# A fused RWKV and mixture-of-experts kernel: three weight splits and the sort move ahead of the second expand group

## The chip, the core and the metric

The kernel runs on one core of one Trainium2 chip. A core has five engines that each work through a queue of their own in order: TensorE (PE in the profile, with its weight loads as PEld), VectorE (DVE), ScalarE (ACT), GpSimd (POOL) and SyncE (SP), which here only starts transfers. Engines wait for each other by semaphores. The metric is device time in microseconds, the median of several runs.

## The reference

```python
def _attn_ref(r, k, v, w, u):            # batch 4, heads 8, seq 768, head_dim 48
    for t in range(S):
        cur = np.einsum('bhd,bhe->bhde', u[None] * kt, vt)
        y[:, :, t] = np.einsum('bhd,bhde->bhe', rt, state + cur)
        state = wt[:, :, :, None] * state + np.einsum('bhd,bhe->bhde', kt, vt)

def _moe_ref(x, w_gate, w1, w2):         # 3072 tokens of 384, 8 experts, hidden 1024
    logits = x @ w_gate
    expert_idx = np.argmax(logits, axis=1)
    ...
    for e in range(E):
        xe = x[expert_idx == e]
        out[expert_idx == e] = gate_w * (np.maximum(xe @ w1[e], 0.0) @ w2[e])
```

A recurrence over 768 steps gives 3072 token rows of 384. Each row goes to the one expert with its largest logit, and the result is scaled by that expert's probability.

## The kernel before

**Two stages.** The first stage works through 24 blocks of the recurrence (`iteration`), turns their outputs into token rows, computes the logits of finished groups (`logit_mm`, `gate`), numbers the rows within their expert (`rank` on TensorE, `place` on VectorE) and writes each block's 128 rows with an indirect transfer from GpSimd into a table `xs`, one region per expert (`scatter`, L603). The second stage goes through the experts one after the other. The busiest expert so far is chosen early (`choose`) and taken first; the order of the other seven is found by `sort_experts` (L632 to L637) after the last block has been ranked, for it needs the final counts (`base`, L580).

**One expert.** Its rows come back from `xs` (`rows_of`, `load_rows`, L260) and are transposed (L300). `expand` (L311) makes one of eight hidden slices of 128: nine TensorE products (three depth slices j, each as high x high, high x low and low x high parts) into one PSUM bank. ScalarE then writes the rectified high part (`hh`, L313), VectorE the rest (`hl`, L314). `contract` (L325) multiplies the eight slices by w2. The first expert's rows are taken in two parts: `ua`, the first 256 rows, known early, and `ub_`, the next 208, which can only be loaded when all blocks have been scattered.

**Splits.** A weight piece arrives by SyncE as 128 x 1536 numbers. `split_part` cuts 512 columns of it into two parts: ScalarE copies the high part (L237), VectorE subtracts to get the low part (L239). `side()` takes the next split from a list; when a piece is done, `feed()` lets SyncE load the next one. The six w1 splits of an expert come in the order set in `feed`:

```python
for k, p in ((0, 0), (0, 2), (1, 1), (0, 1), (1, 0), (1, 2)):
    sides.append(("split", e, k, (halfway["st"], st)[k], p, p == (1, 2)[k]))
```

They are called splits 1 to 6 here. Splits 1 to 3 hold the columns of hidden slices f = 0 to 3 (one split for each j), splits 4 to 6 those of f = 4 to 7. Splits 1 to 3 are done before `mm1(ua, 0)`. Splits 7 to 12 are those of w2; the w2 piece of splits 10 to 12 is the one that `feed` starts to load when split 4 is done.

**Order.** The block is inside `tc.manual_schedule` for TensorE, VectorE, ScalarE and GpSimd, and SyncE is ordered by hand as well: each engine does its instructions in the order in which the program names them. So what `side(0)` adds stands in ScalarE's and VectorE's queues just where the call is, between the `hh` and `hl` of the `mm1` calls around it. TensorE has nothing of a split in its queue. The PSUM banks of `expand` go round a list of five (`bk["b"]`): `mm1(ua, 5)` takes the bank of f = 0 again, f = 6 that of f = 1, f = 7 that of f = 2, and TensorE waits there until `hh` and `hl` of the older slice have been read out. `expert_of(order[...])` lets SyncE read the second expert's number; behind it in SyncE's queue stand the loads of `ub_` (which wait for every scatter) and of the second expert's w1 (L224).

**The first part of the first expert.** `mm1(ua, f)` is `expand` for slice f of `ua`. Between the eight of them and `contract` of `ua` there is no other TensorE work; the transpositions of `ub_` stand behind the first of the two contractions (`tick`).

Of the kernel before, what the change touches and what calls it, by code (L numbers as in the profile page):

```python
# [55 lines left out]
def rwkv_moe_kernel(ctx, tc, rkw, vv, ub, wg, wr, w1, w2, out):  # L56
# [34 lines left out]
    def misc(name):  # L91
        return psM.tile([P, BANK], F32, name=name, tag="m")
# [137 lines left out]
    def split_part(t, st, i, p, half="hl", n=3):  # L230
        nm = "w1" if i < 2 else "w2"
        k = 1536 // n
        cs = slice(p * k, (p + 1) * k)
        hi = t[nm, "h"][:, i % 2, cs]
        lo = t[nm, "l"][:, i % 2, cs]
        if "h" in half:
            nc.scalar.activation(hi, st[:, cs], AF.Copy)  # L237
        if "l" in half:
            nc.vector.tensor_tensor(out=lo, in0=st[:, cs], in1=hi.bitcast(F32), op=ALU.subtract)  # L239
# [64 lines left out]
    def expand(wt, f, x, n, hs):  # L304
        hh, hl = h_tiles(n)
        hp = turn("b", n)
        i = 0
        for j in range(3):
            wh, wl = w1v(wt, "h", j, f), w1v(wt, "l", j, f)
            for a, p in ((wh, 0), (wh, 1), (wl, 0)):  # L310
                nc.tensor.matmul(hp, a, x[p][:, j, :], start=(i == 0), stop=(i == 8))  # L311
                i += 1
        nc.scalar.activation(hh, hp, AF.Relu)  # L313
        nc.vector.scalar_tensor_tensor(out=hl, in0=hp, scalar=0.0, in1=hh.bitcast(F32), op0=ALU.max, op1=ALU.subtract)  # L314
        hs.append((hh, hl))
# [252 lines left out]
    def rank(k):  # L568
        G, i, m = k
        oh = ch["r", k][0]  # L570
        t = misc("rank")
        rk = t[:, 0:(m + 1) * E].rearrange("p (b e) -> p b e", e=E)
        ch["rank", k] = rk
        nc.tensor.matmul(rk, one32, ch["base"].unsqueeze(1).broadcast_to([1, m + 1, E]), start=True, stop=False, skip_group_check=True)
        nc.tensor.matmul(rk[:, 0:m], tri, oh, start=False, stop=False, skip_group_check=True)
        for b in range(m):
            nc.tensor.matmul(rk[:, b + 1:], ones, oh[:, b:b + 1, :].broadcast_to([P, m - b, E]),
                             start=False, stop=(b == m - 1), skip_group_check=True)
        ch["base"] = nb = sm.tile([1, E], F32, name="base", tag="base", bufs=3)
        nc.scalar.activation(nb, rk[0:1, m, :], AF.Copy)  # L580
# [12 lines left out]
    def weigh(k):  # L593
        G, i, m = k
        nc.vector.tensor_reduce(out=ch["xr", G][:, i:i + m, DM], in_=ch["r", k][1], axis=AX.X, op=ALU.add)
# [4 lines left out]
    def scatter(G, bs, behind=None):  # L600
        xr = ch["xr", G]
        for b in bs:
            i = nc.gpsimd.indirect_dma_start(out=xsf, out_offset=bass.IndirectOffsetOnAxis(ap=ch["pi", G, b], axis=0),  # L603
                                             in_=xr[:, b, :], in_offset=None, bounds_check=E * NTOK - 1, oob_is_err=False)
            if behind is not None:
                after(i, behind, "TensorE's dense products")
            for k in scat:
                tc.declare_no_dep(i.ins, k, reason="rows of different tokens")
            scat.append(i.ins)
            nc.gpsimd.memset(none, 0.0)  # L610
# [19 lines left out]
    def sort_experts():  # L630
        key = keys()
        nc.vector.tensor_tensor(out=key, in0=key, in1=pen, op=ALU.add)  # L632
        ch["ks"] = ks = sm.tile([1, E], F32, name="ks", tag="ks")
        nc.vector.max(out=ks, in_=key)
        ki = sm.tile([1, E], I32, name="ki", tag="ki")
        nc.vector.tensor_copy(ki, ks)
        nc.vector.tensor_single_scalar(out=order, in_=ki, scalar=E - 1, op=ALU.bitwise_and)  # L637
# [3 lines left out]
    def check_counts():  # L641
        ks = ch["ks"]
        nc.vector.tensor_tensor(out=bad[:, 0:E], in0=ks, in1=capk, op=ALU.is_ge)
        nc.vector.tensor_tensor(out=bad[:, E:2 * E], in0=ks, in1=leastk, op=ALU.is_lt)
        tot = sm.tile([1, 1], F32, name="tot", tag="tot")
        nc.vector.tensor_reduce(out=tot, in_=ch["base"], axis=AX.X, op=ALU.add)
        nc.vector.tensor_single_scalar(out=bad[:, 2 * E:2 * E + 1], in_=tot, scalar=float(NTOK + NTOK * E * (E - 1) // 2),
                                       op=ALU.not_equal)
# [8 lines left out]
    def check_w(i, t, h):  # L657
        th = t[:, h * 768:(h + 1) * 768]
        nc.vector.tensor_reduce(out=wck[:, 2 * i + h, 0:1], in_=th, axis=AX.X, op=ALU.min)
        nc.scalar.activation(th, th, AF.Relu, bias=mone, scale=1.0, accum_out=wck[:, 2 * i + h, 1:2])  # L660
# [129 lines left out]
    def feed():  # L790
        while len(out_) < 3:
            if not todo or todo[0][0] not in eid:
                return
            e, i = todo.pop(0)
            st = load_piece(eid[e], i) if i < 4 else load_w(e - 1)
            out_.append((e, i))
            if i == 0:
                halfway["st"] = st
            elif i == 1:
                for k, p in ((0, 0), (0, 2), (1, 1), (0, 1), (1, 0), (1, 2)):  # L800
                    sides.append(("split", e, k, (halfway["st"], st)[k], p, p == (1, 2)[k]))
            else:
                for p in range(3 if i < 4 else 2):
                    sides.append(("split" if i < 4 else "check", e, i, st, p, p == (2 if i < 4 else 1)))

    def side(limit=E):
        if sides and sides[0][1] <= limit:
            kind, e, i, t, p, done = sides.pop(0)
            if kind == "split":
                split_part(wts[e % 2], t, i, p)  # L810
            else:
                check_w(e - 1, t, p)
            if done:
                out_.remove((e, i))
                feed()
# [33 lines left out]
    with tc.manual_schedule(engines={ET.PE, ET.DVE, ET.Activation, ET.Pool}):  # L849
# [6 lines left out]
        ua, z = ch["ua"], NB - 1  # L856
# [27 lines left out]
        def mm1(u, f):  # L884
            expand(wts[u["e"] % 2], f, u["x"], u["n"], u["hs"])
# [7 lines left out]
        penalty()  # L893
        scatter(last, (0, 1, 2))
        mm1(ua, 0)
        rank(kb)
        weigh(kb)
        place(kb)
        scatter(last, (3,))
        side(0)  # L900
        mm1(ua, 1)
        side(0)
        mm1(ua, 2)
        side(0)
        sort_experts()
        eid[1] = expert_of(order[0:1, 0:1])
        ub_ = rows_of(HB, HA, 0)
        feed()
        for f in range(3, 8):
            mm1(ua, f)  # L910
            side(0)
            if f == 5:
                check_counts()
        actx.close()
# [299 lines left out]
```

## Time and profile before

| what | us |
|---|---|
| median of 3 runs | 391.16 (390.44 to 392.19) |
| the profiled execution | 389.0 |
| its span, first to last instruction | 387.3 |

Times of rows count from the start of the span. A row of the timeline gives the start, the duration (of all of them, where several are merged), engine, line, operation, tiles and count, and in brackets the idle time of the engine before it with what ended it. Ends of TensorE's products are modelled in the profile, the ends of the other engines are recorded.

### The profile page before, as it was taken

What the parts mean: (1) busy time and instruction counts of PE and PEld (TensorE: products, weight loads), DVE (VectorE), ACT (ScalarE), POOL (GpSimd) and SP (SyncE); (2) the same over time, 40 slices, a digit from 0 to 9 for tenths busy, and PEclk for the clock granted to TensorE, in tenths of its full rate; (3) what the DMA queues carried; (4) which work ended last, traced back from release to release, by engine and by line L of the source; (5) the groups of instructions that cost most, each with busy time, mean ns of one, the idle gap of its engine ahead of it and who ended that gap; (6) DMA issues with size and microseconds to landing.
All of it is one profiled execution on the core that took longest, in us unless ns stands there. A gap on an engine that the chain in (4) does not pass through costs nothing.

```text
span 387.3 us, 11609 instructions
## 1 busy us (share of the span) xinstructions
PE 360.6 (93%) x4644; PEld 326.1 (84%) x4645; DVE 261.6 (68%) x451; ACT 196.0 (51%) x516; POOL 143.8 (37%) x195
## 2 busy tenths in 40 slices
PE   7988999999998896999999999999999999999991
PEld 5666777777776675998998999999999999999990
DVE  8789999989998436595665376476476585782410
ACT  3665666566666234374454355465565563751200
POOL 5577688788887171111000130130130262124021
PEclk9999999999999696999999999999999999999996
DMA  7997777677768125977444554754764665811001
GB/s 205 261 276 215 225 209 225 202 218 220 221 179 278 50 111 146 284 244 239 117 164 162 151 155 149 224 161 154 226 172 146 208 164 187 248 70 40 20 19 41
DMA packets 38021, 67.63 MB, mean 175 GB/s; under 512 B 8141, under 2 KB 19714, under 8 KB 37962
## 3 DMA queue, kind: packets, MB, share of 16 engines
q1 hardware_dynamic: 31658, 57.33, 50.2%
q0 software_dynamic: 6304, 9.50, 7.7%
q8 instruction: 38, 0.62, 0.7%
q14 instruction: 21, 0.17, 0.1%
HBM read 55.34 MB, written 11.64 MB: 173 GB/s over the span
## 4 chain that ended last, share of the span: by engine, by line
PE 80%; DVE 7%; ACT 4%; issue 3%; POOL 2%; another core or an unknown queue 1%; DMA 1%; POOLq 0%; DVEq 0%; ACTq 0%
PE N L311 15%; PE N L325 14%; PE cell L311 7%; PE mM L311 6%; PE N L994 6%; PE cell L994 4%; PE mM L994 3%; PE yp L489 3%; PE yp L479 3%; PE ap L464 2%; DVE kh L368 2%; PE U L499 2%; PE N L300 2%; PE ap L527 2%; PE wrm L142 2%
## 5 line engine op out<-in xcount | busy, mean ns | idle before, releaser
L275 POOL DMA_INDIRECT out_dram<-ot,gi x16 | 22.2, 1391 | 104.0 <-issue 71.7
L275 POOL DMA_INDIRECT out_dram<-ort,gi x13 | 15.5, 1195 | 76.9 <-issue 19.3
L325 PE MATMUL N<-w2h,hh 128*128 128x384 f32 (+4 forms) x104 | 35.9, 345 | 0.0
L314 DVE SCALAR_TENSOR_TENSOR hl<-N,hh 128x256 fp32r<-128x256 f32 (+8 forms) x38 | 19.8, 522 | 23.7 <-ACT hh L313 21.9
L325 PE MATMUL N<-w2l,hh 128*128 128x384 f32 (+4 forms) x104 | 35.0, 337 | 0.0
L325 PE MATMUL N<-w2h,hl 128*128 128x384 f32 (+4 forms) x104 | 35.0, 337 | 0.0
L239 DVE TENSOR_TENSOR w2l<-wst,w2h 128x512 fp32r<-128x512 f32 x48 | 32.1, 687 | 4.1 <-ACT w2h L237 3.6
L239 DVE TENSOR_TENSOR w1l<-wst,w1h 128x512 fp32r<-128x512 f32 x48 | 33.1, 690 | 1.4 <-ACT w1h L237 1.0
L387 POOL TENSOR_TENSOR rk<-rkwt 112x512 f32<-112x512 f32 x24 | 30.6, 1275 | 7.8 <-DMA rkwt<-in_rkw_dram 7.8
L603 POOL DMA_INDIRECT xs<-xr,pi x24 | 24.7, 1028 | 23.8 <-issue 7.3
L313 ACT ACTIVATE hh<-N 128x256 fp32r<-128x256 f32 (+8 forms) x38 | 17.6, 464 | 27.0 <-PE N L311 22.4
L360 DVE TENSOR_TENSOR_SCAN suf<-rkwt,cell 112x536 f32<-112x536 f32 x24 | 30.4, 1267 | 0.5
L237 ACT ACTIVATE w2h<-wst 128x512 fp32r<-128x512 f32 x48 | 28.5, 625 | 3.5 <-DMA wst<-in_w_dram 3.5
L351 DVE TENSOR_TENSOR_SCAN pre<-rkwt,cell 112x536 f32<-112x536 f32 x24 | 30.2, 1259 | 0.2 <-DMA rkwt<-in_rkw_dram 0.2
L237 ACT ACTIVATE w1h<-wst 128x512 fp32r<-128x512 f32 x48 | 29.8, 623 | 0.2 <-ACT x L301 0.2
L393 POOL TENSOR_TENSOR rh<-rkwt,pre 112x512 f32<-112x512 f32 x24 | 28.9, 1203 | 2.3 <-DVE pre L351 2.0
L311 PE MATMUL N<-xh,w1h 128*128 128x440 f32 (+6 forms) x84 | 28.8, 343 | 0.0
L311 PE MATMUL N<-xh,w1l 128*128 128x440 f32 (+6 forms) x84 | 28.6, 341 | 0.0
L311 PE MATMUL N<-xl,w1h 128*128 128x440 f32 (+6 forms) x84 | 28.6, 340 | 0.0
L368 DVE TENSOR_TENSOR kh<-rkwt,suf 112x512 f32<-112x512 f32 x24 | 28.4, 1181 | 0.0
L430 ACT ACTIVATE at<-id,ct 128x64 f32<-128x64 f32 x96 | 25.3, 343 | 0.1
L373 DVE COPY_PREDICATED at<-cmask,ap 128x512 f32<-128x512 int32 x24 | 17.6, 735 | 10.2 <-PE ap L464 7.6
(200 smaller groups left out, 967.5 us busy)
## 6 DMA issues: line engine op xcount, KB each, us to landing
wst<-in_w_dram SPq DMA_DIRECT2D x48, 256.0 KB
wst<-in_w_dram SPq DMA_DIRECT2D x16, 768.0 KB
rkwt<-in_rkw_dram SPq DMA_DIRECT2D x72, 96.0 KB
rkwt<-in_rkw_dram SPq DMA_DIRECT2D x24, 238.0 KB
vt<-in_vv_dram SPq DMA_DIRECT2D x48, 96.0 KB
wck_t<-in_wr_dram SPq DMA_DIRECT2D x6, 768.0 KB
rkwt<-in_rkw_dram SPq DMA_DIRECT2D x12, 224.0 KB
xg<-xs SPq DMA_DIRECT2D x4, 579.0 KB
```

The source lines that it names most:

```text
L237: nc.scalar.activation(hi, st[:, cs], AF.Copy)
L239: nc.vector.tensor_tensor(out=lo, in0=st[:, cs], in1=hi.bitcast(F32), op=ALU.subtract)
L275: i = nc.gpsimd.indirect_dma_start(out=out[:, :], out_offset=bass.IndirectOffsetOnAxis(ap=t.bitcast(I32)[0:rows.shape[0], q, 1:2], axis=0) ...
L311: nc.tensor.matmul(hp, a, x[p][:, j, :], start=(i == 0), stop=(i == 8))
L325: nc.tensor.matmul(op, a[:, cs], w2v(wt, w, f), start=(i == 0), stop=(i == 23))
L351: nc.vector.tensor_tensor_scan(out=d["pt"][:, 0, 0:NW], data0=d["w"], data1=cell[:RP, 0:1].broadcast_to([RP, NW]), initial=1.0, op0=ALU.mu ...
L360: nc.vector.tensor_tensor_scan(out=suf[:, ::-1], data0=d["w"][:, ::-1], data1=cell[:RP, 0:1].broadcast_to([RP, NW]), initial=1.0, op0=ALU. ...
L368: nc.vector.tensor_tensor(out=d["kh"], in0=d["k"], in1=d["suf"][:, :, 3:SEG], op=ALU.mult)
L387: nc.gpsimd.tensor_tensor(out=d["rk"], in0=d["r"], in1=d["k"], op=ALU.mult)
L393: nc.gpsimd.tensor_tensor(out=d["rh"], in0=d["r"], in1=d["pre"][:, :, 1:C + 1], op=ALU.mult)
L430: nc.scalar.activation(d["at"][:, h // NQ, h % NQ, :], id2, AF.Copy, scale=d["ct"][:, h:h + 1])
L994: nc.tensor.matmul(pp, w, a, start=(i == 0), stop=(i == 23))
```

## The change

The three calls of `side(0)` that stood around `mm1(ua, 1)` and `mm1(ua, 2)` (splits 4 to 6) now stand together right behind `mm1(ua, 0)`, ahead of `rank(kb)`, `weigh(kb)`, `place(kb)` and the last `scatter`. `sort_experts`, the reading of the second expert's number, the load of `ub_` and the `feed` that follows now come ahead of `mm1(ua, 1)` in every engine's order. `mm1(ua, 1)` and `mm1(ua, 2)` have no split behind them any more; from f = 3 on the splits stand as before.

```diff
         scatter(last, (0, 1, 2))
         mm1(ua, 0)
+        for _ in range(3):
+            side(0)
         rank(kb)
         weigh(kb)
         place(kb)
         scatter(last, (3,))
-        side(0)
-        mm1(ua, 1)
-        side(0)
-        mm1(ua, 2)
-        side(0)
         sort_experts()
         eid[1] = expert_of(order[0:1, 0:1])
         ub_ = rows_of(HB, HA, 0)
         feed()
-        for f in range(3, 8):
+        for f in range(1, 8):
             mm1(ua, f)
-            side(0)
+            if f > 2:
+                side(0)
             if f == 5:
                 check_counts()
```

## Rows read from the trace of the kernel before

**Rows 1.** The page: busy time, share of the span and count.
```profile
PE 360.6 (93%) x4644; PEld 326.1 (84%) x4645; DVE 261.6 (68%) x451; ACT 196.0 (51%) x516; POOL 143.8 (37%) x195
```

**Rows 2.** Stretches: us; busy PE, PEld, DVE, ACT, POOL; granted clock; DMA share, GB/s.
```profile
145.10:149.70 4.60, 0.89 (x4) 0.49 (x4) 1.47 (x5) 1.59 (x5) 1.84 (x4) 0.93 0.58 151
149.70:156.00 6.30, 6.30 (x27) 5.86 (x28) 5.62 (x18) 3.56 (x9) 0.00 (x0) 0.51 0.49 163
156.00:161.10 5.10, 5.10 (x35) 5.06 (x34) 2.84 (x6) 2.14 (x5) 0.00 (x0) 1.00 0.97 306
```

**Rows 3.** Waits, 140 to 153: total, times, longest.
```profile
PE N L311 <- ACT w1h L237: 3.5, 2, 2.8
```

**Rows 4.** Timeline of TensorE.
```profile
141.63 0.17 PE L577 MATMUL rank<-oh,ones 128*128 128x8 bf16 x1
142.81 0.40 PE L311 MATMUL N<-x,w1h 128*128 128x256 f32 x2
143.88 0.40 PE L311 MATMUL N<-x,w1h 128*128 128x256 f32 x2
...
144.82 0.28 PE L311 MATMUL N<-x,w1l 128*128 128x256 f32 x1
145.79 0.50 PE L311 MATMUL N<-x,w1h 128*128 128x256 f32 x2 [0.69 <-ACT w1h L237]
149.70 0.80 PE L311 MATMUL N<-x,w1h 128*128 128x256 f32 x2 [2.80 <-ACT w1h L237]
```

**Rows 5.** Timeline of ScalarE.
```profile
141.44 0.38 ACT L313 ACTIVATE hh<-cell 128x256 fp32r<-128x256 f32 x1 [0.27 <-PE cell L311]
145.05 0.17 ACT L580 ACTIVATE base<-rank 1x8 f32<-1x8 f32 x1 [3.22 <-PE N L311]
145.12 0.61 ACT L237 ACTIVATE w1h<-wst 128x512 fp32r<-128x512 f32 x1
148.74 0.38 ACT L313 ACTIVATE hh<-N 128x256 fp32r<-128x256 f32 x1 [3.01 <-remote]
```

**Rows 6.** Timeline of VectorE.
```profile
145.77 0.69 DVE L239 TENSOR_TENSOR w1l<-wst,w1h 128x512 fp32r<-128x512 f32 x1 [0.15 <-ACT w1h L237]
149.16 0.42 DVE L314 SCALAR_TENSOR_TENSOR hl<-N,hh 128x256 fp32r<-128x256 f32 x1 [2.70 <-ACT hh L313]
151.22 0.15 DVE L614 SCALAR_TENSOR_TENSOR key<-base,kofs 1x8 f32<-1x8 f32 x1
151.97 0.16 DVE L637 TENSOR_SCALAR order<-ki 1x8 int32<-1x8 int32 x1
```

**Rows 7.** Chain that ended last, in order of time: start, us, what.
```profile
156.94 4.17 PE N L325 x24
```

**Rows 8.** Timeline of GpSimd and SyncE.
```profile
131.30 0.38 POOL L268 COPY gi<-xg 128x2 int32<-128x2 int32 x1
146.39 0.97 POOL L603 DMA_INDIRECT xs<-xr,pi  x1 [0.50 <-issue]
127.67 0.34 SPq L260 DMA_DIRECT2D xg<-xs  x1
153.25 0.88 SPq L260 DMA_DIRECT2D xg<-xs  x2
154.37 3.10 SPq L224 DMA_DIRECT2D wst<-in_w_dram  x6
```

**Rows 9.** Scatter line L603, whole span: issue to landing.
```profile
DMA to landing us min/median/max: 4.1/5.4/5.9
```

**Rows 10.** Waits of TensorE, 156 to the end.
```profile
PE N L300 <- DVE xl L302: 0.9, 1, 0.9
PE N L983 <- ACT oT L1001: 0.6, 1, 0.6
```

**Rows 11.** Stretches at the end of the first stage.
```profile
122.00:125.10 3.10, 1.58 (x25) 1.20 (x22) 2.81 (x5) 1.67 (x6) 2.94 (x5) 1.00 1.05 360
125.10:128.50 3.40, 3.40 (x60) 2.36 (x62) 0.98 (x3) 0.64 (x3) 0.00 (x0) 0.51 0.23 73
```

## The prediction

> **What bounds the kernel now.** The page comes first: TensorE is busy for 93% of the span [rows 1], so a change can only pay where TensorE stands still or runs slowly. The stretches show where that is [rows 2]. From 145.1 to 149.7 it is busy for 0.89 of 4.60 us. From 149.7 to 156.0 it is busy all the time, but at a granted clock of 0.51, the lower of its two levels (1.2 GHz). From 156 on it has the full clock, and until the end of the span it waits only twice, 1.5 us in all [rows 10]. What this place gives back should therefore reach the end, as long as later loads keep up.
>
> The waits name the cause: TensorE's expand line stands 3.5 us for a high part of w1 [rows 3]. The timeline of TensorE shows which product [rows 4]: slices f = 1 to 3 end at 144.82 + 0.28 = 145.10, and f = 4 then takes its three depth slices one by one, the first at 145.79 and the second at 149.70, each behind ScalarE's split. These are splits 4 to 6. ScalarE's timeline shows why they are late [rows 5]: behind the `hh` of f = 0 (141.44, done at 141.82) stands `base`, which is held for 3.22 us until 145.05; split 4 comes behind it at 145.12; then the `hh` of f = 1 is held for 3.01 us until 148.74, and split 5 comes behind that. The splits themselves wait for nothing: their weights are there.
>
> The two holds are odd. The product that `base` reads ends at 141.63 + 0.17 = 141.80 by its row [rows 4], yet `base` is released at 145.05 [rows 5], about when slices 1 to 3 have gone through. The `hh` of f = 1 reads a slice that by its rows has ended by 142.81 + 0.40, and gets it at 148.74, released by something that the trace can't name. I can't explain this and carry it as an unknown.
>
> **The change part by part.** No instruction is added or removed; TensorE's own queue is the same up to its last product.
>
> *Splits 4 to 6 go ahead of `base`.* ScalarE can start them at 141.82. One high part takes 0.61 [rows 5] and one low part 0.69 [rows 6], and VectorE is the slower: 141.82 + 0.61 + 3 x 0.69 = 144.5. That is 0.6 before f = 4 wants the first of them at 145.10, so they cost TensorE nothing, covered by slices 1 to 3. Without that cover each us of lateness would be a us of TensorE's. What goes is this: one slice takes 143.88 - 142.81 = 1.07 at full clock [rows 4], four of them 4.28, and they now take from 145.10 to 156.94, where the contraction begins [rows 7], that is 11.84. The stall and the low clock together cost 7.56, the most that can come back here.
>
> *What is late next on ScalarE and VectorE.* Behind the splits now stand `base`, `weigh`, `place` and the sort, and behind these the `hh` and `hl` of f = 1. TensorE needs that pair out before f = 6, which takes the same bank. Slices 4 and 5 fill 145.10 to 147.24; from there on lateness counts. The sort is 151.22 to 152.13, 0.91 [rows 6]; ranking takes three VectorE operations of about the 0.15 of that row, 0.5. I bound the rest by both readings of the odd holds:
>
> (a) Signals come at once. VectorE is free of splits at 144.5, has placed at 145.0, sorted at 145.9 and written `hl` of f = 1 (0.42 [rows 6]) at 146.3, ahead of 147.24. TensorE runs through: f = 7 ends at 145.10 + 4.28 = 149.38. VectorE still has seven `hl` (0.42), six low parts of w2 (0.69) and four check operations (0.15), 7.7 in all without overlap, until 153.6. The first contraction takes 4.17 [rows 7] and would end at 153.55; its last eighth, 0.5, needs the last low part, so it ends at 153.6 to 154.1.
>
> (b) Signals come as late as now. The `hh` of f = 1 starts at 148.74, its `hl` ends at 149.16 + 0.42 = 149.58, and f = 6 and 7 end at 149.58 + 2.14 = 151.72. VectorE's 7.7 now run from 149.16 to 156.8. The contraction ends between 151.72 + 4.17 = 155.9 and 156.8 + 0.5 = 157.3; I take 156.6, since neighbouring operations overlap a little. Against 156.94 + 4.17 = 161.11 that gives 4.5.
>
> A rule of the Trainium skill speaks for the first: by "Perfetto Trace Analysis", section "Per-engine timelines", a product's signal goes out once PSUM has acknowledged its bytes, and the end shown is only an estimate from its size. By it alone the sum would be that of (a); the 3.22 us of [rows 5] do not agree, unless the products truly end later than shown, which is a rival below.
>
> *The rows of `ub_`.* In (a) the transpositions behind the first contraction meet their rows. The last scatter goes out at 146.39 now, with 0.50 of idle time ahead of it [rows 8]; `place` comes no later, so 145.9 to 146.4. It lands 4.1 to 5.9 later, median 5.4 [rows 9]. SyncE has the second expert's number by then and loads the rows; the first part's rows took 131.30 - 127.67 = 3.63 from issue to first use [rows 8]. The sum is 146.15 + 5.4 + 3.63 = 155.2, with ends at 153.6 and 155.9. So (a) gives 161.11 - 155.2 = 5.9, at best 7.0 (contraction), at least 5.2. In (b) these rows are hidden behind the contraction.
>
> *The loads.* The w2 piece behind split 4 goes out some 3 us earlier, between the scatters. The second expert's first w1 load follows the rows: 154.37 now, some 1 us earlier then. Its first use comes about 5 us earlier, and the trace does not show how much slack there is. If ScalarE has to wait for it, TensorE has four free banks, some 4 us, to go on; I take nothing, and as a bound 2 us.
>
> The forecast stands between (b) and (a), 4.5 and 5.9: 5.2. The profiled execution would go from 389.0 to 383.8; the runs' median is 2.2 higher, and 391.16 - 5.2 = 386.0.
>
> **The rivals.** *The clock falls again.* It fell after the idle stretch at 145.1, and at 125.1 after 1.58 busy of 3.10; then it stayed at 0.51 for 3.4 us [rows 11] and the other time for some 6.3 [rows 2]. In (b) TensorE stands from 147.24 to 149.58, in (a) some 1 to 2 us ahead of the transpositions. A fall of 3.4 costs half of it, 1.7, one of 6.3 costs 3.1: the gain is 3.5 or 2.1, 387.7 to 389.1. "TensorE: Matmul & The Clock Gate", Part 1, in the Trainium skill says that the throttled state is the default and that activity lifts it; the two falls agree.
>
> *The splits are not what held TensorE.* If its products really end when their signals come, TensorE is at work until 148.7, and f = 4 cannot be done before. Four slices from there end at 153.0 at full clock, a gain of 3.9; at the low clock until 156, at 156.7, a gain of 0.3. So 387.3 to 390.9. For it: nobody else explains the holds. Against it: no TensorE row covers 146.9 to 149.7.
>
> *The rows come sooner*, since the w2 load no longer runs beside the last scatter: the full 7.0 or a little more, 383.8 to 384.9.
>
> *Slower.* The w2 load now goes ahead of the last four scatters in the transfer queues, and all rows of `ub_` wait for the last scatter. From 157.5 on as the time at which these rows load (161.11 less 3.63), each us is a us lost. The piece is 0.79 MB, and 306 GB/s moved around 158 [rows 2], so it alone can put the scatter off by 2.6, from 152.3 to 154.9. It would take twice that to lose anything; then 392 to 395.
>
> **How the numbers follow.** The forecast's own case (gain 4.5 to 5.9, 385.3 to 386.7) has 0.47, the clock 0.22, splits not to blame 0.15, rows sooner 0.09, slower 0.07. The range goes from 383.9 to 390.0: it leaves out the slower case, the worst of the third and a little below. A measurement here tells about 0.5% from nothing, 1.96 us: faster means under 389.2, slower over 393.1. The first case, the fourth, nearly all of the second and half of the third make 0.83 for faster; the rest of these and a mild form of the last make 0.12 for same, 0.05 for slower.
>
> **What would show it.** Right: no TensorE wait for L237 between 141 and 157; splits 4 to 6 on ScalarE before `base`; full clock from 139 to at least 153; the contraction of `ua` starting at 149.4 to 151.8; the first transposition of `ub_` at 155 to 157. Wrong: a TensorE idle gap of over 3 us in front of f = 6, a clock of 0.5 after 149, a first transposition later than 158, or a wait for w1 of the second expert after 160.

## The result, and the profile after

The change makes the kernel faster by 1.2%: the ratio of its time to that of the kernel before is 0.988 (95% interval 0.983 to 0.993), from 12 runs of each. Applied to the 391.16 us of the prediction that is 386.5 us (384.6 to 388.3). The ratio leaves out runs more than 1.5% above the fastest of their kernel, so it stands on 4 of the 12 runs of the change and 10 of the 12 of before; over all runs the medians are only 0.4 us apart (390.65 and 391.06). Two further sets of runs, taken later for the experiments, gave 0.989 (0.980 to 0.997) and 0.990 (0.983 to 0.996); the means over all runs of the three sets lie 1.9, 2.7 and 4.6 us below those of the kernel before, the same way each time, though only the third difference is clear of the spread of its runs.

The profiled execution took 386.8 us with a span of 385.0, against 389.0 and 387.3. The page of the profile after, its line of busy time:

```profile
PE 355.8 (92%) x4645; PEld 321.9 (84%) x4645; DVE 259.9 (68%) x451; ACT 195.6 (51%) x516; POOL 144.7 (38%) x195
```

TensorE has the same products and is busy 4.8 us less [rows 1]; its mean granted clock was 0.995, where it was 0.974. Not all of this is the change's doing: the execution of before had low clock in the first stage too [rows 11], this one had none there. The stretches of before, again by the clock of the span (us; busy PE, PEld, DVE, ACT, POOL; granted clock; DMA share, GB/s):

```profile
145.10:149.70 4.60, 3.51 (x25) 2.97 (x24) 2.50 (x11) 0.64 (x2) 3.02 (x7) 1.00 0.82 249
149.70:156.00 6.30, 5.67 (x42) 5.54 (x41) 4.67 (x14) 5.12 (x13) 0.57 (x2) 1.00 0.56 163
156.00:161.10 5.10, 5.10 (x30) 4.58 (x30) 2.90 (x8) 0.68 (x3) 1.17 (x2) 1.00 0.98 324
```

The idle stretch is nearly gone (3.51 busy of 4.60, against 0.89 [rows 2]), and the clock stays at its full level, 2.4 GHz, where it was at 0.51. The waits of TensorE from 140 to 154 (total, times, longest; "issue" is time in which the engine waited for nothing that the profile shows):

```profile
PE N L311 <- issue: 1.3, 4, 0.4
PE N L311 <- DVE order L637: 0.4, 1, 0.4
```

No wait for L237 is left; it was 3.5 us [rows 3]. L637 is the last operation of the sort, which these products do not read, so that name does not tell what the 0.4 us waited for. The timeline of TensorE:

```profile
143.49 0.39 PE L574 MATMUL rank<-base,one 1*128 1x16 f32 x2 [0.17 <-issue]
...
147.85 0.29 PE L311 MATMUL N<-x,w1h 128*128 128x256 f32 x1 [0.17 <-issue]
148.58 0.28 PE L311 MATMUL N<-x,w1h 128*128 128x256 f32 x1 [0.44 <-issue]
149.31 0.36 PE L311 MATMUL N<-x,w1l 128*128 128x256 f32 x1 [0.45 <-DVE order L637]
150.01 0.41 PE L311 MATMUL N<-x,w1h 128*128 128x256 f32 x2 [0.34 <-issue]
150.74 0.28 PE L311 MATMUL N<-x,w1l 128*128 128x256 f32 x1 [0.33 <-issue]
...
154.07 0.34 PE L325 MATMUL N<-w2h,hh 128*128 128x384 f32 x1
...
158.64 0.34 PE L300 MATMUL N<-ident,xg 104*128 104x104 f32 x2
```

The first row is the last block's ranking product. The same three events in the timeline of before:

```profile
141.27 0.39 PE L574 MATMUL rank<-base,one 1*128 1x16 f32 x2 [0.17 <-issue]
...
156.78 0.34 PE L325 MATMUL N<-w2h,hh 128*128 128x384 f32 x1
...
160.95 0.34 PE L300 MATMUL N<-ident,xg 104*128 104x104 f32 x2
```

The ranking product is a good zero, since TensorE's queue ahead of it is the same in both kernels: in this execution it comes at 143.49, in that of before at 141.27. So the first stage happened to take 2.2 us longer here, and the net 2.3 us of the spans hides a larger local gain. (Over the ten profiled executions of this document whose kernel moves nothing ahead of that product, it comes at 141.00 to 148.57: the spread ahead of the place is larger than the whole gain.) From that zero the first contraction starts 10.6 us later (154.07), where it took 15.5 (156.78); the first transposition of `ub_` comes 15.2 us later (158.64), where it took 19.7 (160.95). The local gain is 4.5 us. What remains of the span behind that transposition is 226.4 us in both.

The rows also show what is not in order yet: the products of f = 4 go out some 0.7 us apart from 147.85 to 150.74, with 1.7 us of idle time in all. ScalarE's timeline shows the late signals again:

```profile
143.91 1.66 ACT L237 ACTIVATE w1h<-wst 128x512 fp32r<-128x512 f32 x3
147.88 0.17 ACT L580 ACTIVATE base<-rank 1x8 f32<-1x8 f32 x1 [2.31 <-PE N L311]
150.88 0.94 ACT L313 ACTIVATE hh<-N 128x256 fp32r<-128x256 f32 x3 [2.83 <-PE N L311]
```

Splits 4 to 6 are through before `base`. But `base` comes 4.4 us after the start of its ranking product (3.8 before [rows 4, 5]), and the `hh` of f = 1 comes at 150.88. The timeline of GpSimd and SyncE:

```profile
139.33 1.04 POOL L603 DMA_INDIRECT xs<-xr,pi  x1 [3.62 <-ACT x L301]
...
149.23 0.97 POOL L603 DMA_INDIRECT xs<-xr,pi  x1 [1.10 <-issue]
...
145.29 0.39 SPq L227 DMA_DIRECT2D wst<-in_w_dram  x1
152.34 0.88 SPq L260 DMA_DIRECT2D xg<-xs  x2
153.46 3.08 SPq L224 DMA_DIRECT2D wst<-in_w_dram  x6
```

The first two rows are the first and the last of eight scatters that go out in a row. The last one is 5.7 us behind the ranking product, against 5.1 before [rows 8]; the rows of `ub_` are loaded at 152.34 and are there when the contraction ends.

### The profile page after: what moved, and what is told of

Its sections match the earlier page's. It is cut to its first block, busy times and chain, and to the rows that moved or that the text cites. A ratio compares the mean times of both kernels' runs of the same rounds, so it can differ in the third digit from the quotient of the medians.

```text
span 385.0 us, 11610 instructions
## 1 busy us (share of the span) xinstructions
PE 355.8 (92%) x4645; PEld 321.9 (84%) x4645; DVE 259.9 (68%) x451; ACT 195.6 (51%) x516; POOL 144.7 (38%) x195
## 4 chain that ended last, share of the span: by engine, by line
PE 78%; DVE 6%; DMA 5%; issue 4%; ACT 3%; POOL 1%; SPq 1%; POOLq 0%; DVEq 0%; ACTq 0%
PE N L325 14%; PE N L311 14%; PE cell L311 7%; PE mM L311 6%; PE N L992 6%; PE cell L992 4%; PE mM L992 3%; DMA rkwt<-in_rkw_dram 3%; PE U L499 2%; PE yp L489 2%; PE ap L464 2%; PE yp L479 2%; PE N L300 2%; PE wrm L142 2%; PE kp L516 2%
## 5 line engine op out<-in xcount | busy, mean ns | idle before, releaser
L275 POOL DMA_INDIRECT out_dram<-ort,gi x13 | 15.6, 1196 | 71.8 <-issue 19.4
L603 POOL DMA_INDIRECT xs<-xr,pi x24 | 25.0, 1043 | 28.7 <-PE yp L489 8.2
L237 ACT ACTIVATE w2h<-wst 128x512 fp32r<-128x512 f32 x48 | 28.7, 630 | 5.0 <-DMA wst<-in_w_dram 5.0
L237 ACT ACTIVATE w1h<-wst 128x512 fp32r<-128x512 f32 x48 | 29.6, 623 | 0.2 <-ACT x L301 0.2
L368 DVE TENSOR_TENSOR kh<-rkwt,suf 112x512 f32<-112x512 f32 x24 | 27.2, 1133 | 0.0
```

The costliest lines, as they stand in the source:

```text
L275: i = nc.gpsimd.indirect_dma_start(out=out[:, :], out_offset=bass.IndirectOffsetOnAxis(ap=t.bitcast(I32)[0:rows.shape[0], q, 1:2], axis=0) ...
L368: nc.vector.tensor_tensor(out=d["kh"], in0=d["k"], in1=d["suf"][:, :, 3:SEG], op=ALU.mult)
```

## The experiments

Two questions were open: which part of the change gives the gain, and what makes the signals late. The four kernels of the first group ran on one chip; the kernel before took 392.0 us there.

**The splits alone.** The sort, the number and the load of `ub_` go back behind f = 2; the splits stay ahead of `rank(kb)`.

```diff
         scatter(last, (3,))
+        mm1(ua, 1)
+        mm1(ua, 2)
         sort_experts()
...
-        for f in range(1, 8):
+        for f in range(3, 8):
             mm1(ua, f)
-            if f > 2:
-                side(0)
+            side(0)
```

> Only splits 4 to 6 move ahead of the last block's ranking; the sort, the second expert's number and the load of ub_ stay behind slice f = 2, as before. Theory 1 (the splits are what TensorE waited for): no wait of TensorE for L237 at f = 4, the contraction of ua starts 10 to 11 us after the last ranking product starts (15.5 before, 10.6 with the whole change), and the time is within 0.3% of the whole change, since the rows of ub_, 2 to 3 us later, are still hidden behind the first contraction. Theory 2 (the earlier sort and rows are what pays): the contraction starts as early, but the first transposition of ub_ waits for its rows, and the time is that of the kernel before within 0.5%.

385.78 us; ratio 0.989 (0.982 to 0.995). It was run again beside the second group: 387.08 us, 0.990 (0.983 to 0.997).

> Only splits 4 to 6 moved, beside the whole change on one chip. Theory 1 (the splits alone pay and the sort's place is hidden): within 0.4% of the whole change. Rival (the earlier sort costs something, for it stands ahead of hl of f = 1 to 3 on VectorE): 0.4 to 1% below the whole change.

**The sort alone.** The splits go back between the slices.

```diff
         mm1(ua, 0)
-        for _ in range(3):
-            side(0)
         rank(kb)
...
         feed()
+        side(0)
         for f in range(1, 8):
             mm1(ua, f)
-            if f > 2:
-                side(0)
+            side(0)
```

> Only the sort, the number and the load of ub_ move ahead of slice f = 1; splits 4 to 6 stay between the slices. Theory 1: TensorE waits at f = 4 for L237 as before, 3 us or more, and the w2 load behind split 4 now stands in SyncE's queue behind the rows of ub_, which wait for the last scatter: it goes out at least 5 us later than before, the second half of the first contraction waits for it, and the time is 2 to 4 us above the kernel before. Theory 2: 3 to 5 us below the kernel before, as the whole change.

391.38 us; ratio 0.996 (0.989 to 1.002), so no difference is shown. The loss of 2 to 4 us that the expectation named did not come: the w2 load goes out at 151.60 (146.49 before) and ScalarE waits 1.73 us for it, but the first transposition is only 0.9 us later behind the ranking product than before. TensorE's waits, 140 to 162, and two stretches:

```profile
PE N L311 <- ACT w1h L237: 3.0, 2, 1.6
PE N L311 <- DVE order L637: 0.8, 1, 0.8
```

```profile
145.10:149.10 4.00, 0.89 (x3) 0.48 (x3) 1.68 (x9) 1.17 (x4) 2.06 (x4) 1.00 0.22 85
149.10:155.90 6.80, 6.33 (x27) 5.89 (x28) 5.50 (x14) 4.05 (x10) 0.00 (x0) 0.50 0.63 194
```

The stall for L237 is there as before, and the clock falls behind it as before. The two experiments together put the gain on the splits: they give it alone, on two chips, and none is shown for the sort, neither alone (where the interval has room for up to 1.1%) nor on top (0.988 to 0.990 with it, 0.989 to 0.990 without).

**The ranking behind f = 3.** If the ranking product or the instructions waiting for it made the signals late, f = 1 to 3 would be free of that here.

```diff
         for _ in range(3):
             side(0)
+        for f in range(1, 4):
+            mm1(ua, f)
         rank(kb)
...
         feed()
-        for f in range(1, 8):
+        side(0)
+        for f in range(4, 8):
             mm1(ua, f)
-            if f > 2:
-                side(0)
+            side(0)
```

> As the whole change, but the last block's ranking, its scatter, the sort and what follows stand behind slice f = 3. Theory A (the late signals follow the ranking product): hh of f = 1 to 3 come within 0.5 us of the end of their slices, no idle TensorE ahead of f = 6, the contraction starts some 9 us after the first slice ends and the time is 1 to 3 us below the whole change unless the rows of ub_, 3 us later, take it back. Theory B (they follow from what the transfers do at that time, the eight scatters above all): the signals of f = 1 to 3 are 2 us or more late as in the whole change, wherever the ranking stands.

390.28 us; ratio 0.998 (0.993 to 1.003). ScalarE's timeline:

```profile
148.34 1.66 ACT L237 ACTIVATE w1h<-wst 128x512 fp32r<-128x512 f32 x3
153.22 0.94 ACT L313 ACTIVATE hh<-N 128x256 fp32r<-128x256 f32 x3 [3.22 <-remote]
```

The `hh` of f = 1 is late though no ranking stands ahead of it. The ranking is not the cause. The gain is missing from the ratio, but not from the place: the first transposition comes 19.1 us after the first scatter (162.14 less 143.00), as soon as in the whole change (19.3 to 20.7) and 4.7 us sooner than before (160.95 less 137.11 is 23.8), and the rest of the span is 226.6 us. What this execution lost, it lost ahead of its first scatter, which came 5.9 us later than before, in work that the edit does not touch. Whether that explains the twelve runs stays open.

**The scatters behind f = 7.** All eight scatters, with the load of `ub_` behind them, wait for the last product of slice 7 (`ch["mm"]` names the last product that was issued).

```diff
-        scatter(last - 1, range(GRP), ch["lc"])
...
-        scatter(last, (0, 1, 2))
...
-        scatter(last, (3,))
         sort_experts()
...
+        scatter(last - 1, range(GRP), ch["mm"])
+        scatter(last, (0, 1, 2, 3))
+        eid[1] = expert_of(order[0:1, 0:1])
+        ub_ = rows_of(HB, HA, 0)
+        feed()
```

> As the whole change, but the last eight scatters and the load of ub_ wait for the last product of slice f = 7. Theory B (scatters in flight hold TensorE's signals): base is released within 0.5 us of the end of the ranking products, hh of f = 1 to 3 within 0.5 us of their slices, and f = 7 ends some 9 us after the first slice. Theory A (the ranking product is the cause) or any cause inside TensorE: base is held 3 us or more as in the whole change. The time itself is some 8 to 14 us longer by both, since the rows of ub_ come only after all the scatters.

397.02 us, two runs; ratio 1.017 (1.005 to 1.029). ScalarE's timeline and TensorE's:

```profile
145.21 1.67 ACT L237 ACTIVATE w1h<-wst 128x512 fp32r<-128x512 f32 x3
146.77 0.15 ACT L580 ACTIVATE base<-rank 1x8 f32<-1x8 f32 x1
146.85 0.39 ACT L313 ACTIVATE hh<-N 128x256 fp32r<-128x256 f32 x1
147.85 0.39 ACT L313 ACTIVATE hh<-N 128x256 fp32r<-128x256 f32 x1 [0.62 <-PE N L311]
```

```profile
169.54 0.61 PE L300 MATMUL N<-ident,xg 104*128 104x104 f32 x2 [12.16 <-DMA xg<-xs]
```

Every signal comes at once, and TensorE goes from the ranking product (145.06) to the contraction (153.00) without a gap, in 7.9 us. The rows of `ub_` are then 12.16 us late, and that is the loss. On this chip, then, as far as one profile of each kernel shows, late signals go with the scatters in flight: the three kernels above that send them in a row beside the slices have them (and so has the whole change, run on this chip later), the one that holds them back has not.

The second group moved the scatters, beside the whole change once more; the kernel before took 390.7 us there.

> The whole change once more, on the same chip as the three below. Both theories: the splits pay, so 0.3 to 1.2% below the kernel before. It is the measure for the others.

389.99 us; ratio 0.989 (0.980 to 0.997). The stretches of its profiled execution, of 393.2 us, show something that the first profile of the change did not (the third run below shows it too, in an execution of 388.0 us):

```profile
152.90:156.70 3.80, 1.44 (x10) 1.23 (x10) 0.64 (x3) 0.71 (x3) 1.31 (x4) 1.00 0.82 299
156.70:160.10 3.40, 3.40 (x19) 3.40 (x18) 3.40 (x10) 2.61 (x8) 0.00 (x0) 0.50 0.39 101
```

TensorE is idle for 2.4 us in slice 4, and then the clock goes to 0.50 for 3.4 us. The contraction starts 12.3 us after the ranking product, not 10.6.

**Four scatters one block earlier**, and **all eight behind f = 0**:

```diff
+        if n == NB - 2:
+            scatter(G - 1, range(GRP))
         if n >= 0:
             pool_diag(n + 1)
...
-        scatter(last - 1, range(GRP), ch["lc"])
```

> The whole change, with the first four of the last eight scatters issued one block earlier, while GpSimd waits in block 22; the last four stay. If each scatter in flight holds TensorE's signals for a share of the 7.2 us, the hold behind the first slice shrinks to 3 to 4 us, hh of f = 1 comes before f = 5 ends, TensorE does not stand ahead of f = 6 and that place gives 2 to 3 us; the other half of the hold then falls into block 23, where TensorE, VectorE and ScalarE wait for each other at every step, and costs 1 to 3 us there. Time: between 2 us below the whole change and the same. If the hold does not depend on how many scatters are in flight, it stays 7 us and nothing changes.

```diff
         mm1(ua, 0)
+        scatter(last - 1, range(GRP), ch["mm"])
+        scatter(last, (0, 1, 2))
```

> The whole change, with all of the last eight scatters held until the last product of slice f = 0, some 3 to 4 us later. If the scatters cause the hold, it starts 3 to 4 us later too: the transposes, base of the ranking and hh of f = 1 and 2 come at once, f = 6 and 7 find their banks free, and the hold falls on hh of f = 3 and later, for which the contraction then waits. The rows of ub_ land 3 to 4 us later, about when the first contraction ends or up to 2 us behind it. Time: within 0.5% of the whole change. If the hold follows the ranking, hh of f = 1 is 3 us or more late as before.

Four scatters earlier: 394.11 us, ratio 1.009 (1.005 to 1.014), a loss, where the same or up to 2 us less than the whole change was expected. They go out at 138.23 to 143.10, beside a block of the first stage. The stretches there and behind, in the profiled execution of 398.1 us:

```profile
138.20:143.10 4.90, 3.39 (x67) 2.34 (x67) 0.00 (x0) 0.49 (x1) 4.21 (x8) 0.79 0.32 121
143.10:149.00 5.90, 3.90 (x55) 2.93 (x56) 1.88 (x5) 1.48 (x4) 0.91 (x4) 0.50 0.10 36
```

The clock is low from 141 to 161. TensorE's timeline beside the first four scatters, and ScalarE's beside them and beside the last four:

```profile
140.25 0.35 PE L464 MATMUL ap<-rh,kh 48*64 48x64 f32 x6 [0.40 <-issue]
140.99 0.48 PE L464 MATMUL ap<-rh,kh 64*64 64x64 f32 x4 [0.39 <-issue]
141.71 0.47 PE L464 MATMUL ap<-rh,kh 64*64 64x64 f32 x3 [0.23 <-issue]
```

```profile
144.23 0.49 ACT L455 ACTIVATE xT<-N 128x384 f32<-128x384 f32 x1 [5.54 <-PE N L527]
...
157.95 0.38 ACT L313 ACTIVATE hh<-N 128x256 fp32r<-128x256 f32 x1 [0.88 <-PE N L311]
```

Beside the first four, TensorE's products go out some 0.7 us apart behind "issue", and ScalarE gets the transposed block at 144.23, 1.2 us after the last of its products by their rows (142.11 + 0.90). The last four run beside f = 1 to 3, at the low clock all along, and have neither: `base` comes 1.95 us after its ranking product, and the `hh` of f = 1 at 157.95, 0.1 us after its slice. So in one execution four scatters in a row came once with late signals and once without.

Behind f = 0: 389.85 us, ratio 1.003 (0.999 to 1.007), not within 0.5% of the whole change as expected. The late signals only move: the `hh` of f = 1 and 2 are prompt, for those of f = 4 and 5 (152.21, 155.16) ScalarE stands idle 3.46 and 2.05 us, and the contraction waits 2.0 and 1.7 us for what comes behind them.

**Four scatters in a row.** The last four wait for the last product of slice 7, 1 or 2; the first four stay. These ran on two other chips. The edit for slice 1 (the lines that name the product are left out):

```diff
-        scatter(last, (0, 1, 2))
...
-        scatter(last, (3,))
         sort_experts()
+        for f in range(1, 2):
+            mm1(ua, f)
+        scatter(last, (0, 1, 2, 3), ch["mm"])
         eid[1] = expert_of(order[0:1, 0:1])
```

> The whole change, with the first four of the last eight scatters where they are and the other four (with the load of the second part's rows behind them) held until the last product of slice 7. If the late signals come from scatters in flight and their length goes with the number of scatters, the stretch of late signals begins 4.2 to 4.3 us after the first scatter is issued, as in every run, but lasts about half of 7.3 us, 3.5 to 4; the first contraction then starts 8.5 to 9.5 us after the last ranking product (7.9 with all eight held, 10.6 in the whole change). If the length is a fixed penalty, whatever the number, it lasts some 7 us again and the contraction starts 10 us or more after. If the last four alone are to blame, it does not appear before slice 7 is through. The time of the whole run should be above the kernel before by 2 to 8 us in any case, since the last four scatters and the rows behind them are no longer hidden.

392.73 us, two runs; ratio 1.012 (0.979 to 1.046). GpSimd's timeline, first and fourth scatter, and ScalarE's:

```profile
136.85 1.04 POOL L603 DMA_INDIRECT xs<-xr,pi  x1 [3.61 <-ACT x L301]
...
140.74 0.97 POOL L603 DMA_INDIRECT xs<-xr,pi  x1 [0.22 <-issue]
...
149.40 1.51 POOL L603 DMA_INDIRECT xs<-xr,pi  x1 [7.61 <-PE N L311]
```

```profile
142.94 0.15 ACT L580 ACTIVATE base<-rank 1x8 f32<-1x8 f32 x1
143.00 0.36 ACT L313 ACTIVATE hh<-N 128x256 fp32r<-128x256 f32 x1
```

With four scatters there are no late signals here, not half of them as one theory had it; the contraction starts 7.9 us after the ranking product. The rows of `ub_` are then 7.09 us late.

> The whole change, with the last four scatters (and the load of the second part's rows behind them) held until the last product of slice 1, so that they go out about 7 us after the first four began, when these have landed or nearly so, in place of right behind them. If the late signals need more than four scatters in flight at once, they are gone or last under 2 us: base and the writes of slices 1 to 3 come within 1 us of their products, TensorE runs through slices 4 to 7, and the first contraction starts 7.6 to 8.5 us after the last ranking product (10.6 in the whole change). The last scatter then goes out about 1 us later than in the whole change and its rows set the next step: the first transposition of the second part comes 17.5 to 18.5 us after the first scatter (19.5 in the whole change), so the time is 0 to 2 us under the whole change's, 0.984 to 0.989 of the kernel before. If it is the fifth scatter and what follows that hold the signals, however far behind the first four they go, they are held from some 8 us after the first scatter on, base comes in time, and the contraction comes no sooner than in the whole change.

> The same with the last four scatters held until the last product of slice 2, about 8 us after the first four began. By the count in flight the late signals are gone whatever happens with slice 1, and the contraction starts 7.6 to 8 us after the last ranking product. The rows come 1 us later than with slice 1: first transposition 18.5 to 19.5 us after the first scatter, so the time is that of the whole change to within 1 us. If the last four scatters hold the signals by themselves, products from slice 3 on are held, and the contraction starts over 10 us after the last ranking product.

387.43 us and 387.47 us; ratios 0.998 (0.994 to 1.003) and 1.004 (1.000 to 1.007), against 386.72 us of the kernel before. ScalarE's timeline and TensorE's with the pause behind slice 1:

```profile
143.66 0.15 ACT L580 ACTIVATE base<-rank 1x8 f32<-1x8 f32 x1
143.75 0.38 ACT L313 ACTIVATE hh<-N 128x256 fp32r<-128x256 f32 x1
...
161.56 0.63 ACT L237 ACTIVATE w1h<-wst 128x512 fp32r<-128x512 f32 x1 [1.49 <-DMA wst<-in_w_dram]
```

```profile
155.21 0.40 PE L300 MATMUL N<-ident,xg 104*128 104x104 f32 x2 [0.98 <-DMA xg<-xs]
```

By the profile this is what was expected: prompt signals, the contraction 7.9 us after the ranking product, the first transposition 13.3 us after it. Some 1 us is given back behind it (the span goes on for 227.5 us, not 226.4, and ScalarE waits there for w1 of the second expert). The times show no gain, where 0.984 to 0.989 was expected of the pause behind slice 1, and the kernel before is itself 3 to 6 us faster here than on the other occasions. The last run was the control for that:

> The whole change a third time. In the runs beside the two kernels with the pause between the scatters, the kernel before took 386.7 us at the median, 4 to 5 us less than on the other occasions, and the pause gained nothing against it, though in the profiles the step from the first scatter to the first transposition was 6 to 7 us shorter. This run is the control. If the late signals are part of every execution and the pause is what removed them, they are in this profile again: base is released over 2 us after the ranking product, the contraction starts over 10 us after it, and the first transposition comes 19.5 to 21 us after the first scatter. If they come and go with the chip, base is released at once here too wherever the kernel before is fast (about 387 us), and the ratio is then 0.995 to 1.0; where the kernel before takes 390 to 392 us, they are there and the ratio is 0.985 to 0.992.

386.97 us; ratio 0.990 (0.983 to 0.996); the kernel before took 392.75 us, on the chip of the first group. ScalarE's timeline and two stretches:

```profile
147.12 0.17 ACT L580 ACTIVATE base<-rank 1x8 f32<-1x8 f32 x1 [0.92 <-PE N L311]
150.80 0.94 ACT L313 ACTIVATE hh<-N 128x256 fp32r<-128x256 f32 x3 [3.52 <-remote]
```

```profile
143.40:151.70 8.30, 5.94 (x47) 5.62 (x47) 4.20 (x16) 3.01 (x9) 5.05 (x10) 1.00 0.72 217
151.70:155.20 3.50, 3.50 (x19) 3.50 (x18) 3.47 (x12) 2.89 (x8) 0.00 (x0) 0.51 0.34 86
```

The late signals are there, and the clock falls. This run was not on the chip of the pauses, so it can't tell whether the pause removed the late signals there or whether that chip has none with eight scatters either. One number leans to the second: at a mean granted clock of 0.990 or 0.991, the six runs of the kernel before on the chip of the pauses have a median of 386.3 us, the six on the other chips whose clock is on record 388.1. That does not show it, and no profile of the kernel before was taken there. So this stays open, and with it whether the pause is worth anything.

The kernels that leave the ranking and the first stage where they are, side by side, worked out from their timelines (us after the start of the last ranking product; the rest is the span less the first transposition):

| kernel | `base` | first contraction | first transposition | rest of the span |
|---|---|---|---|---|
| before | 3.8 | 15.5 | 19.7 | 226.4 |
| sort alone | 4.5 | 15.7 | 20.6 | 226.3 |
| whole change, three executions | 4.4, 3.0, 3.7 | 10.6, 12.3, 12.3 | 15.2, 16.5, 16.5 | 226.4, 226.3, 226.4 |
| splits alone, two executions | 6.0, 2.9 | 9.8, 10.3 | 14.6, 15.5 | 227.3, 226.3 |
| all scatters behind f = 7 | 1.7 | 7.9 | 24.5 | 228.3 |
| last four behind f = 7 | 1.9 | 7.9 | 19.4 | 228.0 |
| last four behind f = 1, f = 2 | 1.7, 1.7 | 7.9, 7.9 | 13.3, 13.0 | 227.5, 227.4 |

## Why the prediction was right, and where its steps were not

**What held TensorE.** The prediction read the stall as splits 4 to 6 queued behind `base` and `hh`, and that is shown: moved ahead, they take the wait for L237 away, and moved alone they give the gain of the whole change, to within the intervals.

**The size.** The forecast stood at 5.2, between (b) with 4.5 and (a) with 5.9. The profiled execution gained 4.5 at the first transposition, (b) to the tenth, which is luck: the two other executions gained 3.2 (19.7 less 16.5), and the stall stood elsewhere than in (b), as told below. Case (a) never came, so the half of the way towards it was the mis-sized term. The ratio gives 4.7 us (2.9 to 6.5), which covers both. By the rule of the Trainium skill that the prediction named ("Perfetto Trace Analysis", "Per-engine timelines": a product's signal goes out once PSUM has acknowledged its bytes, and its shown end is an estimate), read as if the shown end were the true one, the sum would have been that of (a). The trace of this kernel does not agree with that reading: `base` comes 3.0 to 4.4 us after the start of the ranking product. It comes 1.7 to 1.9 us after it, right behind the splits, in the runs with fewer scatters in flight. The page itself leaves room for late signals, since it calls the shown end an estimate.

**What is late next.** The step that failed is the place of the remaining stall: (b) let TensorE run through f = 4 and 5 and stand ahead of f = 6, from 147.24 to 149.58, for the bank of f = 1. In the trace it stands inside f = 4, 1.7 us in the first execution and 2.4 in the second, "issue" in the waits, and f = 6 then waits for nothing. The contraction still started when (b) said, 10.6 us behind the ranking product (10.5 by (b)): the stall ended 0.8 us sooner (7.5, at 151.02, against 8.3), with one slice of 1.07 more left to do.

**The clock.** "The clock falls again" had 0.22 as a rival. It happened in two of three profiled executions of the change (0.50 for 3.4 us, 0.51 for 3.5), and there the gain is 3.2, inside the 2.1 to 3.5 that the rival gave; neither of the two profiles of the splits alone has it. So it is no other case but a part of this one that comes and goes; by these executions, 0.22 was too little.

**Splits not to blame.** The rival that TensorE's products really end when their signals come is refuted in its outcome. At its best it has the contraction at 153.0, 11.7 us after the ranking product; it comes after 10.6 us in the first execution of the change and after 9.8 and 10.3 with the splits alone. Its mechanism is refuted in part. ScalarE writes f = 1 to 3 in one go from 150.88 on, three writes in 0.94 us, while TensorE needs 1.07 for each slice: f = 3 had ended by some 151.4, so f = 1 by 149.3, and its write still began only at 150.88. So about 1.6 us of that wait, at the least, is not the products'. How the rest divides between late products and late signals the trace doesn't tell.

**Place and rows.** "`place` comes no later" was wrong in the first execution: the last scatter is 0.6 us later behind the ranking product (5.7, against 5.1), since `base` is. In the two others it held (4.8 and 5.0). It cost nothing, as (b) had said: the rows are covered by the contraction. The loads of the second expert cost nothing either: 226.4 us behind the transposition in both.

**The sort.** The prediction gave the earlier sort no price of its own. The runs show none that can be told from nothing: without its move the ratio is the same.

**The marks set.** No wait for L237 and splits ahead of `base` came as named, the full clock in the first execution only: in the two others the clock of 0.5 that was to mean "wrong" is there. The contraction and the transposition came later than their marks (154.07 and 158.64, against 149.4 to 151.8 and 155 to 157), and the second passes the 158 that was to mean "wrong". 2.2 us of that is the longer first stage of this execution; without it they are 151.9 and 156.4, the one at the edge of its mark, the other inside it. Marks should have been set from an event beside the change, not from the start of the span.

## What to carry to other kernels

When an engine is idle for a result, look at the queue ahead of the instruction that makes it: three splits that needed nothing were late only because they stood behind two instructions that did. Moving work that is ready ahead of work that waits can give back the stall and the low clock that follows it, here 3.2 to 4.5 us of 7.6. Price a move by the waits it passes: the sort passed none that TensorE stood in, and brought nothing that the runs show.

## What was not expected of the hardware

Eight indirect scatters in a row go with a delay of what follows from TensorE's products. The `hh` of f = 1 comes 11.6 us after the first scatter began in the kernel before (148.74 less 137.11), 11.8 with the sort alone, 11.5 in the third run of the change, 10.1 and 10.3 with the splits alone, 10.2 with the ranking late, whatever stands ahead of it; with the scatters held back, on the chip of the sort alone, the third run and the ranking late, it comes 0.08 us after `base`. During that time TensorE's own products go out about 0.7 us apart in the first execution of the change (147.85, 148.58, 149.31, 150.01, 150.74); in the two others TensorE stands twice for 1.1 to 1.2 us. Four scatters in a row, and twice four with a pause, showed neither on two other chips. But the number alone does not decide it: on the chip of the second run of the change, the first four of the kernel with four earlier scatters came with both, and its last four with neither. Why scatters do this, and how much of it is late products and how much late signals, is open.

The kernel before took 389.7 to 392.75 us at the median on five occasions and 386.7 on a sixth, on another chip, and neither of the two kernels tried there was faster than it; the whole change itself was not run there. A gain of this size should be measured on more than one chip.
